# Weight transposes in sixteen pieces, one per row tile, and a layer norm gradient shared by two engines

## Chip, cores and metric

One core of one Trainium2 chip. The metric is the device time of one execution in microseconds (us), the median of several. Kernels are compared by a ratio: the mean time of one kernel's fast runs over the mean time of the other's fast runs of the same rounds, so not quite the ratio of the medians quoted. A difference under 2% counts as "the same".

## The reference, cut to what matters

A forward pass and all its gradients: `out = x + A(xn) + B(xn)`, where `xn` is the layer norm of `x` (2048 x 1024, bf16), A a gated long convolution and B a gated MLP (`gate = xn @ Wg`, `up = xn @ Wu`, `h = relu(gate) * up`, `h @ Wd`, with 3584 hidden columns). The change touches the last two phases:

```
out_0 = x + xn * y + h @ Wd                          # output phase
g_xn  = g * y + g_gate @ Wg^T + g_up @ Wu^T          # x gradient phase
out_1 = g + rstd * (g_xn - mean(g_xn) - xn * mean(g_xn * xn))
```

The second line needs `Wg` and `Wu` transposed, and they are brought in by transposing transfers during the output phase.

## The kernel before

The kernel is written in a framework that derives all semaphore waits from the data flow and fixes the order of each engine's instructions while it builds, by a list schedule: of the instructions that are ready in its model, the one earliest in the program goes next. In the traces the entries of an engine or a transfer queue start one after another and wait where they must: from 1412 to 1620 us of the kernel before, the queue waits 39.9 us, in twelve waits, for matmuls to free a buffer of h's pool.

```python
self.p_hT = tc.alloc_tile_pool(name="b_hT", bufs=3, side="right")     # three buffers for h
def tall(self, src, st, name):                                        # transposing load, 128 rows x 3584
    t = self.p_hT.tile([P, self.FT, P], BF16, name=name, tag="hT")
    self.nc.sync.dma_start_transpose(out=t[:], in_=src[st * P:(st + 1) * P, :])
    return t

def out_phase(self, x, xn_d, y_d, h_d, Wg, Wu, out0):
    ...
    for st in range(self.ST):                                         # 16 row tiles
        hT = self.tall(h_d, st, "hT")
        # plain loads on the same queue: ya <- y, xe <- xn, xr <- x   (128 x 1024 each)
        if st < 8:                                                    # a piece of 256 weight rows
            w, wT = (Wg, self.wgT) if st < 4 else (Wu, self.wuT)
            c = (st % 4) * 256
            nc.sync.dma_start_transpose(out=wT[:, :, c:c + 256], in_=w[c:c + 256, :])
        # VectorE: ya = ya * xe + xr
        for ob in range(2):
            # 28 matmuls into ps from hT and wd, then o0 = ps + ya
            ...
        nc.sync.dma_start(out=out0[rows, :], in_=o0[:])

def grad_x(self, g, xn_d, y_d, ug_d, out1):
    for st in range(self.ST):
        # ggT, guT by tall(); gt <- g, gy <- y, xn; gy = gy * gt
        for ob in range(2):
            # 56 matmuls into ps; gx = ps + gy with its sum in m; pr = gx * xn with its sum in m
            ...
        # m[6:8] = -mean(gx), -mean(gx * xn);  m[4] = m[6] * rstd       (three tiny instructions)
        V.tensor_scalar(out=gm[:], in0=gt[:], scalar1=m[:, 4:5], scalar2=None, op0=ALU.add)
        for ob in range(2):
            V.scalar_tensor_tensor(out=gx[:, oc], in0=xn[:, oc], scalar=m[:, 7:8], in1=gx[:, oc], op0=ALU.mult, op1=ALU.add)
            V.scalar_tensor_tensor(out=o1[:, oc], in0=gx[:, oc], scalar=self.rstd[:, st:st + 1], in1=gm[:, oc], op0=ALU.mult, op1=ALU.add)
            nc.sync.dma_start(out=out1[rows, oc], in_=o1[:, oc])
```

## Time and profile before

| | before |
|---|---|
| median of 3 runs | 2009.09 us (2007.18 to 2009.27) |
| span of the profiled run | 2009.4 us |
| first matmul of the output phase, of the x gradient phase | 1412.50, 1614.01 |
| length of the output phase | 201.5 us |
| its 896 matmuls without any gap | 193.4 us |
| tensor engine's waits for hT in it | 5.9 us, three |
| start of the last eviction, and from there to the end of the span | 2000.98, 8.4 us |

An eviction is the VectorE instruction that reads a finished matmul result, half a row tile wide. The tensor engine sets the time (busy 1944.6 us, 97% of the span); the two numbers that the change can move are the output phase's length and the stretch after the last matmul. The prediction shows the lines they come from.

### The profile page before, as it was taken

The page shows a single profiled execution, that of the slowest core. Times are in us where ns is not written, and L with a number is a line of the kernel's source. Part 1 is how long each engine was busy: PE and PEld are TensorE (multiplying, and loading weights), DVE is VectorE, ACT ScalarE, POOL GpSimd, SP SyncE. Part 2 cuts the span into 40 slices and gives each one's busy share as a digit, 9 for nine tenths or more (in the row PEclk, how much of TensorE's full clock was granted, in tenths as well). Part 3 has the DMA queues.
Part 4 walks back from the last instruction along what each step waited for, and adds up shares of the span by engine and source line. Part 5 has one row for each costly group of instructions (what it writes and reads, how often), then busy time and mean ns, then how long its engine had stood idle before and what let it go on. Part 6 is the DMA issues. An engine that isn't in the chain of part 4 may idle for free.

```text
span 2009.4 us, 27247 instructions
## 1 busy us (share of the span) xinstructions
PE 1944.6 (97%) x11022; PEld 916.2 (46%) x11022; DVE 996.6 (50%) x1460; ACT 694.6 (35%) x912; POOL 16.3 (1%) x36
## 2 busy tenths in 40 slices
PE   3999999999999999999999999999999999999998
PEld 1445445444444444444454444444444444444443
DVE  5769678677677756666585650000112222233332
ACT  6455456456447428384564741111000000000000
POOL 2000000000000000000000000000000000000000
PEclk8999999999999999999999999999999999999999
DMA  9864675975674674444655259422999545544551
GB/s 269 220 162 124 157 201 150 217 189 134 156 197 125 189 210 119 130 135 133 191 159 139 81 171 300 163 93 76 213 268 226 148 115 122 127 116 121 125 127 42
DMA packets 614895, 318.32 MB, mean 158 GB/s; under 512 B 449896, under 2 KB 584048, under 8 KB 614768
## 3 DMA queue, kind: packets, MB, share of 16 engines
q1 hardware_dynamic: 613488, 312.38, 59.3%
q0 software_dynamic: 1280, 4.20, 0.6%
q8 instruction: 86, 1.41, 0.3%
q14 instruction: 41, 0.34, 0.0%
HBM read 141.36 MB, written 95.44 MB: 118 GB/s over the span
## 4 chain that ended last, share of the span: by engine, by line
PE 47%; ACT 2%; DMA 1%; SPq 1%; issue 0%; DVE 0%; DVEq 0%
PE ps_x L822 19%; PE ps_w L705 17%; PE ps_o L789 8%; PE ps L65 1%; DMA hT<-h_d 1%; ACT G L69 1%; SPq L781 0%; ACT H L69 0%; ACT K L69 0%; ACT wi L743 0%; ACT B L69 0%; SPq L758 0%; PE pst L280 0%; DVE gx L837 0%; DVE gm L834 0%
## 5 line engine op out<-in xcount | busy, mean ns | idle before, releaser
L705 PE MATMUL ps_w<-ugs,xn_nat 128*128 128x512 bf16 x1792 | 400.2, 379 | 1.1 <-DMA xn_nat<-xn_d 1.0
L595 PEld LDWEIGHTS <-xnT 128*128 128x128 bf16 x1792 | 169.7, 99 | 215.8 <-issue 23.2
L705 PEld LDWEIGHTS <-xn_nat 128*128 128x128 bf16 x1792 | 170.9, 98 | 204.2 <-issue 8.2
L595 PE MATMUL ps_g<-wg,xnT 128*128 128x512 bf16 x896 | 213.6, 387 | 15.4 <-DVE xnT L621 11.4
L705 PE MATMUL ps_d<-g_nat,hs 128*128 128x512 bf16 x896 | 208.6, 381 | 3.6 <-DMA hs<-h_d 3.6
L595 PE MATMUL ps_h<-wdT,goT 128*128 128x512 bf16 x896 | 207.4, 379 | 0.0
L595 PE MATMUL ps_u<-wu,xnT 128*128 128x512 bf16 x896 | 207.3, 379 | 0.0
L789 PE MATMUL ps_o<-wd,hT 128*128 128x512 bf16 x896 | 195.8, 381 | 5.9 <-DMA hT<-h_d 5.9
L822 PE MATMUL ps_x<-wgT,ggT 128*128 128x512 bf16 x896 | 198.6, 379 | 0.0
L822 PE MATMUL ps_x<-wuT,guT 128*128 128x512 bf16 x896 | 198.6, 379 | 0.0
L791 DVE TENSOR_TENSOR o<-ps_o,ya 128x512 bf16<-128x512 f32 x32 | 21.6, 687 | 277.4 <-PE ps_o L789 277.3
L743 ACT CAST wi<-ps_w 128x512 bf16<-128x512 f32 x112 | 65.6, 586 | 233.4 <-PE ps_w L705 230.7
L789 PEld LDWEIGHTS <-hT 128*128 128x128 bf16 x896 | 87.9, 98 | 113.6 <-DMA hT<-h_d 7.4
L824 DVE CUSTOM_DVE_ANT_0 gx<-ps_x,gy 128x512 f32<-128x512 f32 x32 | 22.1, 692 | 229.9 <-PE ps_x L822 229.9
L822 PEld LDWEIGHTS <-ggT 128*128 128x128 bf16 x896 | 87.7, 98 | 105.7
L822 PEld LDWEIGHTS <-guT 128*128 128x128 bf16 x896 | 87.7, 98 | 105.7
L664 ACT CAST gh<-ps_h 128x512 bf16<-128x512 f32 x112 | 65.5, 586 | 191.9 <-PE ps_h L595 120.8
L705 PEld LDWEIGHTS <-hs 128*128 128x128 bf16 x896 | 83.1, 98 | 100.6 <-issue 9.7
L595 PEld LDWEIGHTS <-goT 128*128 128x128 bf16 x896 | 84.1, 98 | 97.8 <-issue 6.1
L291 DVE STREAM_TRANSPOSE flp<-B 128x1024 f32<-128x1024 f32 x48 | 90.2, 1935 | 47.8 <-ACT B L69 47.6
L69 ACT CAST C<-ps 128x1024 bf16<-128x1024 f32 x96 | 96.7, 1016 | 48.4 <-PE ps L65 48.4
L652 DVE SCALAR_TENSOR_TENSOR ru<-ru,ps_u 128x512 bf16<-128x512 bf16 x112 | 76.2, 681 | 64.4 <-PE ps_u L595 52.2
(156 smaller groups left out, 1714.5 us busy)
## 6 DMA issues: line engine op xcount, KB each, us to landing
ug_d<-ru SPq DMA_DIRECT2D x112, 256.0 KB, 3.5
ugs<-ug_d SPq DMA_DIRECT2D x112, 256.0 KB, 4.4
wg<-in_B_W_gate_dram SPq DMA_DIRECT2D x56, 256.0 KB, 4.7
wu<-in_B_W_up_dram SPq DMA_DIRECT2D x56, 256.0 KB, 3.2
h_d<-ht SPq DMA_DIRECT2D x112, 128.0 KB, 2.2
hs<-h_d SPq DMA_DIRECT2D x56, 256.0 KB, 4.6
out_dram<-wi SPq DMA_DIRECT2D x56, 256.0 KB, 2.1
gt<-in_grad_out_dram SPq DMA_DIRECT2D x32, 256.0 KB, 4.0
```

The costliest lines, as they stand in the source:

```text
L65: self.nc.tensor.matmul(out, lhsT=lhsT, rhs=rhs, start=start, stop=stop)
L69: self.nc.scalar.copy(out=out, in_=in_)
L291: self.nc.vector.transpose(out=df[:, c0:c0 + 32, :], in_=sf[:, c0:c0 + 32, :])
L595: self.nc.tensor.matmul(ps[:], lhsT=xT[:, kt * P:(kt + 1) * P], rhs=w(kt), start=(kt == 0), stop=(kt == self.DT - 1))
L652: nc.vector.scalar_tensor_tensor(out=ru[s][:, 1, :], in0=ru[s][:, 0, :], scalar=0.0, in1=ps[:], op0=ALU.is_gt, op1=ALU.mult)
L664: nc.scalar.copy(out=gh[:], in_=ps[:])
L705: self.nc.tensor.matmul(ps[:], lhsT=lhsT(st), rhs=rhs(st), start=(st == 0), stop=(st == self.ST - 1))
L743: nc.scalar.copy(out=wo[:, d, :], in_=ps[:])
L789: nc.tensor.matmul(ps[:], lhsT=hT[:, kt, :], rhs=self.wd[:, kt, oc], start=(kt == 0), stop=(kt == self.FT - 1))
L791: nc.vector.tensor_tensor(out=o0[:, oc], in0=ps[:], in1=ya[:, oc], op=ALU.add)
L822: nc.tensor.matmul(ps[:], lhsT=T[:, kt, :], rhs=W[:, kt, oc], start=(i == 0), stop=(i == n - 1))
L824: V.tensor_tensor_reduce(out=gx[:, oc], in0=ps[:], in1=gy[:, oc], scale=1.0, scalar=0.0, op0=ALU.add, op1=ALU.add, accum_out=m[:, ob:ob + 1])
```

## The change

Its intent: load the transposed weights in even pieces, one per row tile, so that the transfer queue isn't overloaded in the first half of the output phase; and shorten the last gradient steps by giving a part of them to the idle ScalarE (0.00 us busy in the 386.9 us from 1614.1 to 2001.0).

```diff
-            if st < 8:
-                w, wT = (Wg, self.wgT) if st < 4 else (Wu, self.wuT)
-                c = (st % 4) * 256
-                nc.sync.dma_start_transpose(out=wT[:, :, c:c + 256], in_=w[c:c + 256, :])
+            w, wT = (Wg, self.wgT) if st < 8 else (Wu, self.wuT)
+            c = (st % 8) * P
+            nc.sync.dma_start_transpose(out=wT[:, :, c:c + P], in_=w[c:c + P, :])
 ...
+            w = p_ev.tile([P, D], F32, name="w")
 ...
-            V.tensor_scalar(out=m[:, 4:5], in0=m[:, 6:7], scalar1=self.rstd[:, st:st + 1], ...)
+            V.tensor_scalar(out=m[:, 4:6], in0=m[:, 6:8], scalar1=self.rstd[:, st:st + 1], ...)
-            V.tensor_scalar(out=gm[:], in0=gt[:], scalar1=m[:, 4:5], scalar2=None, op0=ALU.add)
             for ob in range(2):
-                V.scalar_tensor_tensor(out=gx[:, oc], in0=xn[:, oc], scalar=m[:, 7:8], in1=gx[:, oc], ...)
-                V.scalar_tensor_tensor(out=o1[:, oc], in0=gx[:, oc], scalar=self.rstd[:, st:st + 1], in1=gm[:, oc], ...)
+                nc.scalar.activation(out=w[:, oc], in_=xn[:, oc], func=ACT.Identity, scale=m[:, 5:6], bias=m[:, 4:5])
+                V.scalar_tensor_tensor(out=gx[:, oc], in0=gx[:, oc], scalar=self.rstd[:, st:st + 1], in1=gt[:, oc], ...)
+                V.tensor_tensor(out=o1[:, oc], in0=gx[:, oc], in1=w[:, oc], op=ALU.add)
```

More of the change, by code (lines that the diff above doesn't have):

```diff
@@ L830, in grad_x @@
             V.tensor_scalar(out=m[:, 6:8], in0=m[:, 4:6], scalar1=-1.0 / D, scalar2=None, op0=ALU.mult)
-            V.tensor_scalar(out=m[:, 4:5], in0=m[:, 6:7], scalar1=self.rstd[:, st:st + 1], scalar2=None, op0=ALU.mult)
+            V.tensor_scalar(out=m[:, 4:6], in0=m[:, 6:8], scalar1=self.rstd[:, st:st + 1], scalar2=None, op0=ALU.mult)
             o1 = p_ev.tile([P, D], BF16, name="o1")
-            gm = p_ev.tile([P, D], F32, name="gm")
-            V.tensor_scalar(out=gm[:], in0=gt[:], scalar1=m[:, 4:5], scalar2=None, op0=ALU.add)
             for ob in range(2):
                 oc = slice(ob * 512, ob * 512 + 512)
-                V.scalar_tensor_tensor(out=gx[:, oc], in0=xn[:, oc], scalar=m[:, 7:8], in1=gx[:, oc], op0=ALU.mult,
-                                       op1=ALU.add)
-                V.scalar_tensor_tensor(out=o1[:, oc], in0=gx[:, oc], scalar=self.rstd[:, st:st + 1], in1=gm[:, oc],
+                nc.scalar.activation(out=w[:, oc], in_=xn[:, oc], func=ACT.Identity, scale=m[:, 5:6], bias=m[:, 4:5])
+                V.scalar_tensor_tensor(out=gx[:, oc], in0=gx[:, oc], scalar=self.rstd[:, st:st + 1], in1=gt[:, oc],
                                        op0=ALU.mult, op1=ALU.add)
+                V.tensor_tensor(out=o1[:, oc], in0=gx[:, oc], in1=w[:, oc], op=ALU.add)
                 nc.sync.dma_start(out=out1[rows, oc], in_=o1[:, oc])
```

## The prediction

> **What bounds the kernel now.** I looked first at the busy shares, then at the chain that ended last, then at the tensor engine's waits inside the phases that the diff touches, then at the DMA queue's order of issue, and last at the final microseconds. The busy shares and the slices say tensor engine: it is busy 97% of the span and full in every slice but the first and the last.
>
> ```profile
> PE 1944.6 (97%) x11022; PEld 916.2 (46%) x11022; DVE 996.6 (50%) x1460; ACT 694.6 (35%) x912; POOL 16.3 (1%) x36
> ```
>
> So a change that removes no matmul can win only what the tensor engine loses between matmuls, and what runs after the last one. The diff touches the output phase (16 row tiles, from 1412.5 us) and the x gradient phase (16 row tiles, from 1614.0 us). The waits of the window 1412 to 1615 (what waited for what, us in total, times, longest):
>
> ```profile
> PE ps_o L789 <- DMA hT<-h_d: 5.9, 3, 2.6
> ```
>
> and the tensor engine's timeline of the two phases (start, length, what; in brackets the idle time before):
>
> ```profile
> 1412.50 72.68 PE L789 MATMUL ps_o<-wd,hT 128*128 128x512 bf16 x336
> 1486.19 12.26 PE L789 MATMUL ps_o<-wd,hT 128*128 128x512 bf16 x56 [1.00 <-DMA hT<-h_d]
> 1501.05 12.26 PE L789 MATMUL ps_o<-wd,hT 128*128 128x512 bf16 x56 [2.60 <-DMA hT<-h_d]
> 1515.62 98.55 PE L789 MATMUL ps_o<-wd,hT 128*128 128x512 bf16 x448 [2.31 <-DMA hT<-h_d]
> ```
>
> Row tiles 6, 7 and 8 wait for the transposed h; the rest of the phase and the whole x gradient phase have no such wait. How much is lost: evictions of half tiles late in the phase come at 1602.12, 1608.17 and 1614.21, 6.045 us for 28 matmuls, 0.2159 each, so 896 need 193.4 us. The phase took 1614.01 - 1412.50 = 201.5, so 8.1 are lost. The listed idle is 5.9. Idle is counted from a modelled end 0.379 after a matmul's start where the next would have started at 0.216, which adds 0.16 for each stall, 0.5. The other 1.7 lie just after the third stall, in weight loads that come twice as slowly:
>
> ```profile
> 1516.91 0.15 PEld L789 LDWEIGHTS <-hT 128*128 128x128 bf16 x1 [0.28 <-issue]
> 1517.34 0.15 PEld L789 LDWEIGHTS <-hT 128*128 128x128 bf16 x1 [0.27 <-issue]
> ```
>
> Some eight such steps of 0.427 instead of 0.216 make 1.7 us. The same signature follows other stalls (after 2.33 idle at 43.5 us, after 2.23 at 512.4), not every one (not the first two here). I count it to the stall, as likely to vary from run to run; one of the three timed runs was 1.9 us faster than the others.
>
> Why h is late: the DMA queue, in the middle of the eight tiles that carry a weight piece:
>
> ```profile
> 1479.68 4.33 SPq L758 DMA_TRANSPOSE hT<-h_d  x1
> 1484.05 0.58 SPq L775 DMA_DIRECT2D xe<-xn_d  x1
> 1484.67 0.43 SPq L777 DMA_DIRECT2D xr<-in_A_q_dram  x1
> 1485.53 0.35 SPq L792 DMA_DIRECT2D out_dram<-o  x1
> 1485.92 0.42 SPq L773 DMA_DIRECT2D ya<-y_d  x1
> 1486.40 8.76 SPq L781 DMA_TRANSPOSE wuT<-in_B_W_up_dram  x1
> 1495.26 3.59 SPq L758 DMA_TRANSPOSE hT<-h_d  x1
> ```
>
> One round of issuing here takes 1495.26 - 1479.68 = 15.6 us; over the four rounds from 1451.25 to 1509.12 it is 14.5 on average. The matmuls of a row tile take 56 x 0.2159 = 12.1. Three h buffers and the early start carry the queue for three tiles; then 2.4 us are lost per round and become the stalls. From 1515.6, with no piece left, the queue waits for free h buffers instead (39.9 us in twelve waits), and nothing stalls.
>
> After the last matmul: its eviction starts at 2000.98, the last row tile's VectorE work ends near 2006.4, the second store of it starts about then, and the span ends at 2009.4.
>
> ```profile
> 2002.85 0.21 DVE L831 TENSOR_SCALAR m<-m,rstd 128x1 f32<-128x1 f32 x1
> 2002.98 0.74 DVE L837 SCALAR_TENSOR_TENSOR gx<-xn,m,gx 128x512 f32<-128x512 bf16 x1
> 2003.64 0.74 DVE L834 TENSOR_SCALAR gm<-gt,m 128x1024 f32<-128x1024 bf16 x1
> 2004.31 0.74 DVE L837 SCALAR_TENSOR_TENSOR gx<-xn,m,gx 128x512 f32<-128x512 bf16 x1
> 2004.97 1.41 DVE L839 SCALAR_TENSOR_TENSOR o<-gx,rstd,gm 128x512 bf16<-128x512 f32 x2
> ```
>
> Five instructions at a pitch of 0.66 follow the small ones.
>
> [...] here 128 rows of 3584 hold the queue 3.5 us at best and 256 rows 6.9, so the halves add up to the whole.
>
> **The change, part by part.**
> The pieces: eight transposes of 256 rows (7.1 us median for the gate, 8.1 for the up weights) become sixteen of 128, each about the 3.8 median of hT. The queue's total stays (8 x 7.6 = 61, 16 x 3.8 = 61); what changes is that tiles 0 to 7 carry half of it. At one piece per tile a round is 14.5 - 3.8 = 10.7 us, below 12.1. Then h comes on time and the 8.1 us go, all of them: behind this phase the tensor engine runs with no wait to 2001, so an earlier start of the x gradient is an earlier end. I take 7.6, keeping 0.5 for a residue of stall, or half clock elsewhere.
>
> The gradient steps: gm (one instruction of 1024) and two steps with xn (512 each) leave VectorE; two additions (512, fp32, about 0.69) come in; the two others keep their form. Per row tile five large instructions become four. Over fifteen row tiles this is worth nothing, since VectorE is 113 us busy in 387 of this phase. In the last row tile it counts. ScalarE needs the small m values, at 2003.06[...]. Meanwhile gx*rstd + gt, which needs no m, can run; its first half can even go in the 10 us gap before the last eviction, for VectorE's order in the trace isn't program order (gx, gm, gx, o, o against gm, gx, o, gx, o). [...] Both first steps after m: 2.98 + 4 x 0.66 and the tail of the last make 5.7, 0.7 earlier. [...] I take 0.7. [...]
>
> Sum: 7.6 + 0.7 = 8.3 us. 2009.1 - 8.3 = 2000.8.
>
> **Rivals.**
> 1. The queue takes pieces as early as it can, not one per tile. For it: the first two were issued back to back at 1415.59, before the h of tile 3. Then three go first and up to two per tile follow, the round stays 14.5, and the deficit comes back. Against a full return: ahead of tile 6's h stand about 9 pieces of 128 rows where 12 stood, and by tile 8 13 where 16 stood, some 11 us of queue less against an idle sum of 5.9. Worth 2001 to 2005, about one in five.
> 2. The 16 DMA engines are the limit, not the queue. Their share is 1.11 and 1.13 in the windows 1412.5 to 1485.2 and 1485.2 to 1515.6, then 0.66. Weighted by window length that is 80.7 + 34.4 + 65.0 = 180 us of engine time, which in a phase of 193 makes 0.93 when even: lower than what they carried. If landings nevertheless stretch beyond 6.5 us, h has two tiles (24 us) between buffer and need. 2000.8 stays; one in ten that stalls of 2 to 4 us remain.
> 3. The late pieces stand before the x gradient's first transposes (1590.03 and 1602.12 now) or its matmuls. The last piece should be queued around the 14th tile, near 1585, and its columns are read only in the second half of the first x gradient tile. A whole-tile wait would still be met. One in twenty, 2003 to 2006.
> 4. ScalarE's hop eats the tail gain: then 2001.5.
>
> **Range and chances.** [...] Rivals 1 to 3 at half strength leave half the gain: 2005. So 1998.8 to 2005.0. Two per cent would be 40 us; the whole reachable loss is 9, so within 2% is close to sure.
>
> **What would show it.** In the changed profile, the wait of ps_o for hT should be gone and the first ps_x matmul should start near 1606; sixteen transposes of wgT and wuT of 3.5 to 4.5 us should be spread over at least eight tiles. VectorE should have no gm, and the time from the last eviction's start to the span's end should fall from 8.4 to about 7.7. I am wrong if hT stalls stay above 3 us, if ps_x gains a wait for wuT or guT, or if the time stays above 2005 with the stalls gone.

The sum: 7.6 us for the output phase and 0.7 for the tail make 8.3, and 2009.1 - 8.3 = 2000.8. The 0.7 is the case left of three, worked out from the 0.66 us at which VectorE's instructions follow each other in the trace, and it takes for granted that ScalarE has its part in time. The other two cases rested on an estimate of ScalarE's time. The low end of the range, 1998.8, counted on the better of these two and on the luck of the fastest run. That an addition takes about 0.69 us is shown: 687 ns on average for the evictions of 512 columns at L791 in the kernel before, and 692 for the additions themselves in the one after.

## The result, and the profile after

| | before | after |
|---|---|---|
| median | 2009.18 us (4 runs, 2007.18 to 2012.94) | 2007.39 us (4 runs, 2005.30 to 2008.57) |
| ratio, 95% interval | | 0.9988 (0.9970 to 1.0005): the same |
| span of the profiled run | 2009.4 | 2005.6 |
| start of the output phase | 1412.50 | 1408.79 |
| output phase | 201.5 | 201.9 |
| waits for hT | 5.9 | 6.5 |
| last eviction to the end | 8.4 | 8.0 |
| start of the output phase to the end | 596.9 | 596.8 |

The predicted 2000.8 (1998.8 to 2005.0) was missed: most of the 8.3 us expected did not come. The last row says more than the medians: from the start of the output phase, just before the two programs begin to differ, the changed kernel took 0.1 us less. The rest of the 3.8 us between the two spans lies ahead of it. Up to the first weight piece both programs have the same instructions in the same order on every engine, and the lead is already there early. The same small matmul in the tensor engine's timeline, first before, then after:

```profile
105.74 0.23 PE L213 MATMUL ps_sk<-ident,sk_b 128*32 128x128 bf16 x1
```

```profile
103.32 0.23 PE L213 MATMUL ps_sk<-ident,sk_b 128*32 128x128 bf16 x1
```

That is 2.4 of the 3.7 us, from waits and half-rate matmuls in the start-up: up to there the tensor engine's waits add up to 32.6 us before and 31.4 after, and the two groups of 16 matmuls that begin slowly took 5.67 and 6.21 us (at 24.10 and 43.48) before, 4.98 and 5.69 (at 22.95 and 41.59) after. Over the ten kernels profiled, all alike up to there but for the first few plain loads of two of them, the output phase began between 1408.16 and 1412.50. This spread is no effect of the change, so the phases are compared below by their lengths.

The stalls first. The tensor engine's timeline of the output phase after the change:

```profile
1408.79 84.81 PE L788 MATMUL ps_o<-wd,hT 128*128 128x512 bf16 x384
1495.85 3.90 PE L788 MATMUL ps_o<-wd,hT 128*128 128x512 bf16 x11 [2.25 <-DMA hT<-h_d]
1499.97 9.82 PE L788 MATMUL ps_o<-wd,hT 128*128 128x512 bf16 x44 [0.22 <-issue]
1511.78 12.04 PE L788 MATMUL ps_o<-wd,hT 128*128 128x512 bf16 x54 [1.99 <-DMA hT<-h_d]
1526.05 84.78 PE L788 MATMUL ps_o<-wd,hT 128*128 128x512 bf16 x385 [2.23 <-DMA hT<-h_d]
```

There are still three stalls, now at row tiles 7, 8 and 9 instead of 6, 7 and 8, with a stretch of half-rate matmuls after the first of them (11 recorded matmuls in 3.9 us, a few records are missing; the weight loads in it come every 0.427 us instead of 0.216, and the granted clock is 0.50 from 1496.9 to 1500.3). The phase loses 201.9 - 193.4 = 8.5 us, where it lost 8.1. The queue's timeline says why:

```profile
1411.88 16.21 SPq L780 DMA_TRANSPOSE wgT<-in_B_W_gate_dram  x4
1428.13 0.58 SPq L791 DMA_DIRECT2D out_dram<-o  x1
1428.76 0.43 SPq L773 DMA_DIRECT2D ya<-y_d  x1
1429.23 4.08 SPq L758 DMA_TRANSPOSE hT<-h_d  x1
1433.35 0.58 SPq L775 DMA_DIRECT2D xe<-xn_d  x1
1434.05 0.36 SPq L777 DMA_DIRECT2D xr<-in_A_q_dram  x1
1434.45 8.29 SPq L780 DMA_TRANSPOSE wgT<-in_B_W_gate_dram  x2
```

Four pieces go at once, then two after every h, although the program writes one per row tile. As I read the program, a piece waits for nothing but its place in the buffer, which all get at the same moment, so the list schedule takes pieces of later tiles whenever the queue would otherwise be free in its model. No run shows that model itself; the order is seen above, and the first experiment below changes the order alone. From the first of these h transposes to that of tile 9 (1429.23 to 1520.19, six rounds) a round is 15.2 us, more than the 14.5 before, against 12.1 us of matmuls.

The tail did what it was meant to, in part (the timeline of all engines at the end):

```profile
1999.11 0.16 DVE L828 TENSOR_TENSOR m<-m 128x2 f32<-128x2 f32 x1
1999.19 0.74 DVE L836 SCALAR_TENSOR_TENSOR gx<-gx,rstd,gt 128x512 f32<-128x512 f32 x1
1999.85 0.16 DVE L830 TENSOR_SCALAR m<-m 128x2 f32<-128x2 f32 x1
2000.05 0.23 DVE L831 TENSOR_SCALAR m<-m,rstd 128x2 f32<-128x2 f32 x1
2000.36 1.52 ACT L835 ACTIVATE w<-xn,m 128x512 f32<-128x512 bf16 x2 [22.66 <-issue]
2001.21 1.40 DVE L838 TENSOR_TENSOR o<-gx,w 128x512 bf16<-128x512 f32 x2 [0.93 <-ACT w L835]
```

The first half's gx*rstd + gt has gone into the gap before the last eviction, as hoped. The second half's stands between the small m instructions, 0.66 us ahead of the two that ScalarE waits for, and VectorE then sits idle 0.93 us until ScalarE has the first half of w.

### The profile page after: what moved, and what is told of

Its sections match the earlier page's. It is cut to its first block, busy times and chain, and to the rows that moved or that the text cites. A ratio compares the mean times of both kernels' runs of the same rounds, so it can differ in the third digit from the quotient of the medians.

```text
span 2005.6 us, 27089 instructions
## 1 busy us (share of the span) xinstructions
PE 1930.6 (96%) x10817; PEld 915.7 (46%) x11022; DVE 986.3 (49%) x1444; ACT 718.5 (36%) x944; POOL 16.3 (1%) x36
## 5 line engine op out<-in xcount | busy, mean ns | idle before, releaser
L705 PE MATMUL ps_w<-ugs,xn_nat 128*128 128x512 bf16 x1746 | 395.2, 379 | 3.9 <-issue 1.0
L835 ACT ACTIVATE w<-xn,m 128x512 f32<-128x512 bf16 x32 | 24.3, 806 | 568.0 <-issue 317.2
```

What stands on the lines that cost most here:

```text
L705: self.nc.tensor.matmul(ps[:], lhsT=lhsT(st), rhs=rhs(st), start=(st == 0), stop=(st == self.ST - 1))
L835: nc.scalar.activation(out=w[:, oc], in_=xn[:, oc], func=ACT.Identity, scale=m[:, 5:6], bias=m[:, 4:5])
```

## Experiments

The theory: the phase gained nothing because pace, not size, decides, and the pace didn't change; the queue was merely given twice as many pieces half as large and took twice as many per round. Rivals: the 16 DMA engines are too full whatever the order; a smaller piece helps or costs by itself. "Phase" is from the first output matmul to the first x gradient matmul, "tail" from the last eviction's start to the end of the span; both are from one profiled execution of each kernel. All runs but the one with fewer bytes gave correct results.

**One piece per row tile, enforced.** An order edge, with no wait attached, puts each piece behind the same tile's h on the queue.

```diff
+            if st < 3: <as it is>
+            else:
+                with tc.issue_after(self.tall_dma.ins):     # the transfer that tall() issued
                     nc.sync.dma_start_transpose(out=wT[:, :, c:c + P], in_=w[c:c + P, :])
```

> The changed kernel with one thing added: the weight piece of row tile st (from st = 3 on) is queued behind the h transpose of the same tile, so that the queue takes one 128-row piece per row tile instead of up to two. Theory A (the queue ran ahead: two pieces per round make a round of 14.9 us against 12.1 of matmuls): the round falls to about 12.1, set by the matmuls, all 16 pieces are spread over 14 rounds, the waits of ps_o for hT (6.5 us) go to zero, and the output phase, first ps_o matmul to first ps_x matmul, takes 193 to 195 us instead of 201.9. Theory B (the DMA engines are too full whenever pieces and h overlap): the phase stays at 199 us or more with hT waits of 4 us or more. Time: A 1998 to 2002, ratio to before about 0.9955; B about 2007.

Measured: 2000.16 us median of 5, ratio to before 0.9956 (0.9943 to 0.9970). No wait for hT; phase 193.4, tail 7.95. In the tensor engine's timeline the whole phase is one stretch (again with some records missing):

```profile
1408.68 193.55 PE L792 MATMUL ps_o<-wd,hT 128*128 128x512 bf16 x878
1602.07 6.21 PE L826 MATMUL ps_x<-wgT,ggT 128*128 128x512 bf16 x27
```

and in the queue's timeline h transposes follow each other at the matmuls' pace, 12.1 us, with one piece between (plain transfers cut):

```profile
1481.40 3.59 SPq L758 DMA_TRANSPOSE hT<-h_d  x1
...
1486.14 3.94 SPq L784 DMA_TRANSPOSE wuT<-in_B_W_up_dram  x1
...
1493.49 3.60 SPq L758 DMA_TRANSPOSE hT<-h_d  x1
```

Theory A holds, and theory B as stated is out: pieces and h still overlap, with the same bytes and the same pieces, and nothing stalls. This run doesn't tell the queue from the engines, because spreading eases both: the share of the 16 DMA engines (the time that their packets took, which can pass 1) over the stretch with pieces is 1.03, where it was 1.13 in the changed kernel. The half-rate stretch is gone with the stalls: no output matmul lasts over 379 ns, where the longest took 634 in the changed kernel.

**Large pieces, paced.** Pieces of 256 rows, one per two row tiles.

```diff
+            if st % 2 == 0:
+                # w, wT, c as in the changed kernel; from st = 4 on inside issue_after
+                nc.sync.dma_start_transpose(out=wT[:, :, c:c + 256], in_=w[c:c + 256, :])
```

> Pieces of 256 rows as before the change, but one per two row tiles (at even tiles, from tile 4 on queued behind that tile's h). Tells size from pacing. Theory A (only the pace counts): no hT wait, output phase 193 to 195 us, as in the paced run with 128 rows. If the smaller piece is what helps (a long piece holds up the h behind it): waits of 1 to 4 us stay and the phase takes 195 to 199.

Measured: one run, 1999.57 us; no wait for hT, phase 193.4, tail 7.97. Halving the pieces isn't needed at all.

**Small pieces in the old order.** The kernel before, each piece split into two right behind each other, everything else in its old order.

```diff
+                for c in (c, c + P):
+                    # order edges as needed to keep the order of before
+                    nc.sync.dma_start_transpose(out=wT[:, :, c:c + P], in_=w[c:c + P, :])
```

> The kernel before, each 256-row piece issued as two of 128 rows right behind each other, the order of everything else on the queue kept. Measures what halving alone costs. In the changed kernel 16 pieces held the queue 67.3 us in all, in the kernel before 8 held it 62.2. If halves cost more by themselves: total 66 to 68, hT waits 8 to 12 us, phase 204 to 208. If halves add up to the whole and the 67.3 came from other traffic in those rounds: total 61 to 63.5, waits 5 to 7 us, phase 200.5 to 203.

Measured: one run, 2012.15 us; pieces hold the queue 67.8 us in all, hT waits 10.0 us, phase 205.7, tail 8.4. So halving costs by itself: 67.8 against 62.2 us, 4.2 us for each 128 rows instead of 3.9. The paced kernels show a cost of the pieces too (66.7 us in all for sixteen in the run above, 59.5 for eight in the large paced run), but there the sixteen transposes of 128 rows go with shorter transposes of h (50.1 us for the last thirteen against 56.7), so the sum is nearly the same, 116.8 against 116.3, and neither stalls. In the changed kernel this cost stands against what its other order gives (201.9 against 205.7 here), and the two about cancel, by chance. Why a half costs more than half isn't shown by any run.

**Small transfers on another queue.** The kernel before, in its old order, with ya, xe, xr and o issued by ScalarE.

```diff
-            nc.sync.dma_start(out=ya[:], in_=y_d[rows, :])          # likewise xe, xr and the store of o0
+            nc.scalar.dma_start(out=ya[:], in_=y_d[rows, :])
```

> The kernel before, pieces of 256 rows and their order against the h transposes kept by order edges; the four plain transfers of each row tile in the output phase (ya, xe, xr, o) are issued from the ScalarE queue, which does nothing there. The bytes on the 16 DMA engines stay. Theory A (issuing on the one queue is the limit): a round falls from 14.5 to about 12.2 (one h 3.9, one piece 7.9, gaps), waits of ps_o for hT fall from 5.9 to under 1.5 us, phase 193.5 to 196. Theory B (the DMA engines are the limit): transposes take longer in the same measure, the round stays above 13.8 and the phase above 199.

Measured: one run, 2008.80 us; hT waits 7.4 us, phase 203.1. Neither theory as stated. The later rounds did fall, to 12.7 us (tile 4's h at 1455.20, tile 8's at 1506.04), but the first four pieces took 25.9 us for three and 11.3 for the fourth, and 4.7 of the 7.4 us of stalls came as early as tiles 3 and 4, the rest at 6 and 8. The windows (length, busy time of the five engines, granted clock, mean share of the 16 DMA engines, GB/s) show the transfer engines fuller in the second and third stretch than before, where the share was 1.12 to 1.15; in the first, where the three pieces took 25.9 us, it is 1.14, so the share doesn't explain that. First this run, then the four late rounds of the kernel before:

```profile
1411.60:1437.60 26.00, 25.89 (x120) 11.77 (x121) 4.06 (x6) 0.00 (x0) 0.00 (x0) 1.00 1.14 234
1437.60:1455.20 17.60, 16.56 (x77) 7.39 (x77) 2.68 (x4) 0.00 (x0) 0.00 (x0) 1.00 1.25 237
1455.20:1506.00 50.80, 45.77 (x202) 20.06 (x205) 7.75 (x12) 0.00 (x0) 0.00 (x0) 0.97 1.23 281
```

```profile
1451.25:1509.10 57.85, 54.25 (x252) 24.29 (x250) 10.33 (x16) 0.00 (x0) 0.00 (x0) 1.00 1.14 264
```

Here ya took 6.5 us from issue to landing where it took 2.7. The paced kernel, with no stall, has:

```profile
1423.80:1578.00 154.20, 153.46 (x702) 69.97 (x715) 35.29 (x51) 0.00 (x0) 0.00 (x0) 1.00 1.03 243
```

**Fewer bytes, as many transfers.** The kernel before, pieces and h in their old order (in the trace the piece now goes ahead of the store o and of ya), with ya, xe and xr loaded 64 columns wide.

```diff
-            ya = p_ev.tile([P, D], BF16, name="ya")                 # likewise xe, xr
+            ya = p_ev.tile([P, 64], BF16, name="ya")
```

> Wrong result on purpose (out_0). The kernel before, order of pieces and h kept by order edges; ya, xe and xr are loaded 64 columns wide instead of 1024, so the queue issues as many transfers as before but 0.74 MB less per row tile goes over the 16 DMA engines. Theory A (the transposes hold the queue for the same time whatever else moves): one h and one piece stay at about 12.1 us, the round at 14.4, hT waits 5 to 7 us. Theory B (the engines' load lengthens the transposes, seen in the run with the small transfers moved, where the engines' share was 1.23): h and piece fall to 10.8 or less, the round to 13.2 or less, waits to 2 us or less.

Measured: one run, 2008.54 us, out_0 wrong as intended; hT waits 4.7 us, phase 200.3. Again between the two: late rounds of 13.5 us, an h and a piece 11.1 together (12.2 before). So the lighter load goes with about 1 us of a round of 14.5. What holds the rest isn't settled, for the engines' share fell only from 1.14 to 1.05:

```profile
1437.60:1506.00 68.40, 66.02 (x306) 29.60 (x305) 7.12 (x17) 0.00 (x0) 0.00 (x0) 1.00 1.05 228
```

That is about the share of the paced kernel, which has no stall, so the engines' share alone doesn't decide. A transpose of 128 rows holds the queue for 3.5 us at the least even in the x gradient phase (3459 ns for ggT in the kernel before), where the share is 0.47, so an h and two pieces would hold it for some 10.5 us (an estimate) before the four plain transfers; that speaks for the queue, but isn't proof. What the runs show is that easing the queue alone or the engines alone left 7.4 and 4.7 us of stalls, and that sending less per round removes them.

**The pace alone.** The kernel before, its large pieces one per two row tiles, the gradient steps as before; the edit is that of the large paced pieces.

> The kernel before with nothing changed but the pace: its 256-row pieces go one per two row tiles, from tile 4 on behind that tile's h; the gradient steps as before. Theory: the stalls go by the pace alone, output phase 193.4 us, no hT wait; from the last eviction's start to the end 8.4 us as before. Time 2000 to 2002, ratio to before about 0.996. Rival (part of the gain comes from the gradient steps on ScalarE): phase 193.4 but the x gradient phase longer, time 2003 or more.

Measured: 2000.02 us median of 4, ratio 0.9952 (0.9934 to 0.9971); no wait for hT, phase 193.4, tail 8.4. All of the gain in the phase comes from the pace:

```profile
1408.65 193.55 PE L790 MATMUL ps_o<-wd,hT 128*128 128x512 bf16 x896
```

**The tail's order, with pacing.** The second half's gx*rstd + gt goes behind the last m instruction.

```diff
+                with (tc.issue_after(m_last.ins) if ob == 1 else ExitStack()):
                     V.scalar_tensor_tensor(out=gx[:, oc], in0=gx[:, oc], scalar=self.rstd[:, st:st + 1], in1=gt[:, oc], ...)
```

> The paced kernel (one 128-row piece per row tile) with the second half's gx*rstd + gt queued behind the last of the small m values on VectorE, instead of ahead of two of them. Theory: ScalarE's steps start with the m values, so they start 0.66 us earlier and VectorE's step runs beside them; from the last eviction's start to the span's end 7.3 to 7.5 us instead of 7.95. Rival: the final additions still wait for VectorE, not for ScalarE, and it stays at 7.9. Output phase 193.4 as in the paced run. Time 1996 to 2000.

> The same end, with pieces of 256 rows, one per two row tiles. If the size of a piece doesn't matter once paced: output phase 193.4 us, no hT wait, time within 1 us of the same kernel with 128-row pieces. If the 16 longer-held small pieces cost anything beyond the queue: 0.5 to 1.5 us faster than it.

Measured with small pieces: 1998.94 us median of 6, ratio 0.9945 (0.9932 to 0.9959), phase 193.4, tail 7.4. With large pieces: 1999.97 us median of 6, ratio 0.9948 (0.9934 to 0.9962), phase 193.4, tail 7.4. The two can't be told apart in time. The end of the first (timeline of all engines):

```profile
1992.08 0.23 DVE L835 TENSOR_SCALAR m<-m,rstd 128x2 f32<-128x2 f32 x1
1992.21 0.75 DVE L841 SCALAR_TENSOR_TENSOR gx<-gx,rstd,gt 128x512 f32<-128x512 f32 x1
1992.39 1.52 ACT L839 ACTIVATE w<-xn,m 128x512 f32<-128x512 bf16 x2 [22.65 <-issue]
1993.24 1.40 DVE L843 TENSOR_TENSOR o<-gx,w 128x512 bf16<-128x512 f32 x2 [0.28 <-ACT w L839]
```

VectorE's step now lies beside ScalarE's, and the idle time before the additions falls from 0.93 to 0.28. The tail was 8.4 in all five profiled kernels with the old gradient steps, 7.95 to 8.0 in the three with the new, and 7.4 in these two. In time, a tail's half microsecond can't be seen beside runs that spread by 3 to 5 us: all the paced kernels that were timed in rounds lie between ratios of 0.9945 and 0.9956, with overlapping intervals. They are faster than the kernel before clear of noise, and still "the same" by the 2% of this document.

## Why the prediction was wrong, point by point

- **The bound, and what was lost: right.** 8.1 us of loss in the output phase was the correct stake. With no stalls the phase took 193.4 us in five kernels, as worked out, and the half-rate stretch went with the stalls, as I had counted it.
- **The pace: the step that failed.** "At one piece per tile a round is 14.5 - 3.8 = 10.7 us, below 12.1." The arithmetic is right (the paced run has room to wait for the matmuls in each round), but the changed kernel doesn't send one piece per tile. It sent four at once and then two per tile, and a round took 15.2 us, against 12.1 of matmuls. So 6.5 us of waits for h stayed, and of the 8.1 us that were to go none went; with one piece per tile enforced they all went. The place of a line in the program was taken for its place on the queue. The trace of before had the evidence, two pieces back to back ahead of tile 3's h, and I wrote it down under rival 1.
- **Rival 1 named the mechanism and was mis-sized.** I gave it one chance in five and "2001 to 2005", because 13 pieces instead of 16 would stand ahead of tile 8's h, "some 11 us of queue less against an idle sum of 5.9". There were 14, and two terms were missing. First, the remaining two only go ahead of tile 9's h, so the full 16 still stand ahead of something: the deadline moved by one tile, 12.1 us, and so did the work of one round. Second, the same rows hold the queue 67.3 us in small pieces and 62.2 in large ones. In total the loss became 8.5 where it was 8.1.
- **"So the halves add up to the whole": wrong.** They cost 4.2 instead of 3.9 us per 128 rows, shown by the run in the old order. The shortest single durations had been compared, not the sums.
- **Rival 2, the DMA engines, in part.** It was right that an even load fits, at a share of 1.03 over the stretch with pieces and about 0.95 over the phase, where 0.93 was estimated. But I treated engine and queue as alternatives: relieving the queue alone and lightening the engines alone both left stalls. Which of them holds a round at 13.5 us in the latter run stays open.
- **Rival 3: right to be small.** In the changed kernel it couldn't come up, as the last pieces went at 1509.36. In the paced kernel the last piece went at 1570.84, and no x gradient matmul waited.
- **The tail: right in kind, 0.45 instead of 0.7.** ScalarE began 0.08 us after the last m instruction ended (2000.28 to 2000.36), and its two steps took 1.52 us, 806 ns each on average; the author's estimate of these times is cut above. VectorE's order was between the case above and the best case: one half of gx*rstd + gt early, the other ahead of two of the m instructions, so that the m values were ready 2.6 us after the last eviction's start instead of 2.1. Putting it behind them gave the other half microsecond. Rival 4, that the hop eats the gain, didn't come.
- **A reading of the clock that doesn't hold.** The half-rate matmuls at 43.5 us were put down to 2.33 us of idle time. The tensor engine was slow already: the 16 small matmuls just before took 1.86 us (at 39.29, after 6.06 us of idle, at a granted clock of 0.50) where the next 16 of the same kind took 1.06. The cases at 512.4 us (steps of some 0.43 us after 2.23 us of idle time, the granted clock 0.58 from 512.4 to 516, and 8 matmuls in 1.89 us before it) and in the output phase stand.

## What to carry to other kernels

To spread transfers over a phase, it isn't enough to write them spread: a transfer that waits for nothing may be put on its queue early by the scheduler, here the last piece before the h of tile 9 instead of behind that of tile 15, so tie it to something that comes at the pace wanted, and look at the queue's timeline for its real order. When a queue is behind for a stretch, compare the whole of its work with the time up to the last consumer that it serves; fewer items ahead of one consumer can be more ahead of the next. And with effects of a few microseconds, compare the phase that was changed by its length in the trace: the spread of an unrelated phase can be as large as the effect sought.

## What the traces show besides

- Half-rate matmuls (steps of 0.427 us, some eight of them, at a granted clock of 0.54 from 1516.5 to 1520.2 before and 0.50 from 1496.9 to 1500.3 after) followed idle times of 2.31 us in the kernel before and 2.25 in the one after; 2.60 in the one and 2.23 in the other were followed by none. The length of the gap alone doesn't decide; what does, the runs don't settle.
- For a transposing transfer the time for which it holds its queue isn't small against the transfer: 128 rows of 3584 hold the issuing queue 3.5 to 5.3 us of some 5.6 to landing in the kernel before, a plain 256 KB transfer mostly 0.3 to 0.6. Moving the plain transfers to another queue gained nothing in the phase in the run here (203.1 us against 201.5), though late rounds fell from 14.5 to 12.7.
- What splitting a transpose costs, measured in one unchanged order: 62.2 us of queue time for eight transposes of 256 rows, 67.8 for sixteen of 128.
